# Attention and a feed-forward layer on one core: q and k of six batches by casting transfers in place of loads and casts on the engines, with a new order of all operations

## The chip, the cores and the metric

The kernel runs on one core of a Trainium2 chip. The core has five engines with a queue each: TensorE (PE in the profile; its weight loads are PEld), VectorE (DVE), ScalarE (ACT), GpSimd (POOL) and SyncE (SP), and 16 DMA engines that all queues share. Every engine runs its instructions in the order of its queue and waits on semaphores for the others. The metric is the device time of one execution in microseconds (us); smaller is better.

## The reference

Inputs are q, k and v, each of shape (8 batches, 12 heads, 448 rows, 64 columns), and the weights w_in (768 x 2048) and w_out (2048 x 768), all float32.

```python
scores = scale * np.matmul(q, k.transpose(0, 1, 3, 2))
attn = np.maximum(scores, 0.0) ** 2 / S
attn_out = np.matmul(attn, v)
...
x = attn_out.transpose(0, 2, 1, 3).reshape(B * S, H * D)
h = x @ w_in
g = h * (1.0 / (1.0 + np.exp(-1.702 * h)))
out = g @ w_out
```

So there is no softmax: the scores are clipped at zero and squared. The output has 3584 rows of 768 columns.

## The kernel before

All matrix work is in float16 with float32 sums. The work is cut into 24 attention units (8 batches of three units, a unit being two pairs of heads) and 8 feed-forward groups, one for each batch.

The whole order of the work is written out by hand (a planner's output) as a string of some 2,000 words, from line 431 on; `do` (line 404) calls one function for each word, and each engine's queue receives its instructions in the order of the words. A word is a name, its arguments, `@` the PSUM banks it takes, and `:` an engine (`a` ACT, `d` DVE, `p` POOL; some names have an engine as their home, for example the widening `v` POOL). The words that matter here:

- `Lq6`, `Lk6` (`load`, line 94): SP loads q or k of unit 6 in float32 into one staging tile each (pools qst and kst, one buffer). `Q6`, `K6` (`cast`, line 103) cast it on POOL, ACT or DVE into a float16 tile (pools q16 and k16, two buffers) whose two heads of a column block lie side by side. Units 0 and 6 to 23 take this way.
- `jq1`, `jk1` (`load_cast`, line 98): a DMA of POOL's queue loads q or k and casts on the way, as whole rows of 448 columns for each of the two halves, 256 packets in all. Units 1 to 5 take this way. `V3` does the same for v of unit 3 (pool v16, four buffers). `jwa0`, `jwb0` to `jwa3`, `jwb3` (`load_w_in`, line 374) load eight pieces of w_in and `jo0.0` to `jo1.1` (`load_w_out`, line 378) four pieces of w_out, on the same queue, 384 and 1024 packets each.
- `G3` (`sp_gate`, line 384): a small copy on SP that waits for the last piece of w_in, so that SP's later loads start behind it.
- `tq6`, `tk6` (`trans_pe`, line 112): PE turns a unit's q or k by multiplying with an identity matrix: 7 matmuls over the whole array (line 117) where the tile has heads side by side, 14 over half of it (line 122) otherwise. `eq6`, `ek6` (`trans_evac`, line 127) copy the result from PSUM.
- `s5.6@3.0` (`scores`, line 134): scores of unit 5, block 6, into banks 3 and 0; four matmuls of 64 x 64. `r`, `x`: clip (two halves, ACT or DVE) and square. `a5` (`attn_v`, line 164): the product with v, 28 matmuls. `e5.0`, `e5.1`: its two eviction halves into x of the batch (tile xb).
- `f0.14.0@3` (`m1`, line 202): two of the six matmuls of block 14 of the first feed-forward product of group 0. `g0.14` (`m1_gelu`, line 213): ACT reads the bank and writes the gelu into a float32 tile of pool gf, five buffers. `v0.14` (`m1_widen`, line 217): the widening, which scales a gf tile and writes it as float16 into its place in the tile ring, on POOL or DVE. With that the gf buffer is free. Groups 1 to 7 do the first product by a seven-product scheme (`u`, `t`, `b`, `g`, `v` with three arguments: product, copy, addition, gelu, widening).
- `p0.0` (`pair_product`, line 339): 8 matmuls of the second product for rows of the pair of tiles 0 and 1, which read ring blocks 0 to 7 and w_out; `p0.1` reads blocks 8 to 15. `A`, `S`, `T`, `W` are sums of operands on DVE for the seven-product scheme. `h`, `l` evict, `o` and `q26.0.1` store.

Within the first 60 us the order is: units 0 to 2 (batch 0) of the attention while the weights land, then the first feed-forward product of group 0 between the scores of units 3 to 5, then `u1...` and `p0.0`. From there attention of the next batches and feed-forward of the one before run interleaved to the end.

Of the kernel before, what the change touches and what calls it, by code (L numbers as in the profile page):

```python
# [8 lines left out]
F32 = mybir.dt.float32  # L9
# [6 lines left out]
def kernel(  # L16
# [31 lines left out]
    for name, bufs in (("cst", 1), ("kst", 1), ("qst", 1), ("k16", 2), ("q16", 2), ("v16", 4),  # L48
                       ("kT", 3), ("qT", 3), ("at", 15), ("xb", 2),
                       ("T1", 1), ("T2", 1), ("T4", 1), ("gf", 5),  # L50
                       ("as0", 1), ("as1", 1), ("osb", 3)):
        pool(name, bufs)
# [3 lines left out]
    def new(tag, shape, dt, name=None):  # L56
        return pools[tag].tile(shape, dt, name=name or tag, tag=tag)

    def const(name, shape, dt=F16):
        return pools["cst"].tile(shape, dt, name=name)  # L60

    ident = const("ident", [128, 128])
    gate = const("gate", [1, 64])
# [26 lines left out]
    def quad(n, u):  # L90
        b, pr = divmod(u, NP)
        return src[n][b].rearrange("(a i s) (p j) d -> i (s p) a (j d)", a=2, i=NP, j=J)[pr]

    def load(n, u):
        units[u][n + "st"] = new(f"{n}st", [128, 2, S], F32)
        nc.sync.dma_start(out=units[u][n + "st"], in_=quad(n, u))

    def load_cast(n, u):
        x = new(f"{n}16", [128, 2, S], F16)
        nc.gpsimd.dma_start(out=x, in_=quad(n, u))  # L100
        units[u][n + "16"] = x
# [282 lines left out]
    def sp_gate(e, p, i):  # L384
        nc.sync.dma_start(out=gate[0:1, :], in_=win[i][127:128, 0, 0:64])

    with tc.manual_schedule():
# [4 lines left out]
               "G": sp_gate,  # L392
# [29 lines left out]
        def zeros(e, p, n):  # L422
# [8 lines left out]
            "Lq0 Lk0 z9@0 jq1 jk1 I V0 V1 z1 Q0:d z1 z1 z1 z1 z1 z1 tq0@1 K0:d eq0:a tk0@2 ek0 "  # L431
            "tq1@3 jk2 eq1 s0.1@4.5 jq2 s0.4@6.7 s0.5@0.1 r0.1.1 r0.1.0:d s0.0@2.3 jq3 r0.5.1 "
            "r0.5.0:d s0.6@5.4 r0.0.0 r0.0.1:d r0.6.0 s0.2@1.0 x0.5 r0.2.0 s0.3@2.3 tk1@5 r0.2.1 "
            "x0.1 r0.4.0 ek1 jk3 r0.3.0 x0.2 r0.6.1 s1.6@1.0 jwb0 s1.3@6.5 r0.3.1:d r1.6.0 jwa0 "
            "r1.6.1 x0.6 s1.2@2.4 s1.0@3.1 r1.3.0 x0.3 r1.2.0 s1.5@0.6 x0.0 r0.4.1 r1.5.0:d r1.2.1 "
            "s1.1@2.7 r1.0.1 r1.0.0:d tk2@0 r1.1.0 x0.4 s1.4@4.1 r1.3.1 tq2@3 ek2 r1.1.1 a0@2.5 jq4 "
            "eq2 x1.3:a x1.2 jk4 r1.5.1 r1.4.0:d tq3@0 e0.0:a V2 x1.0 s2.3@7.3 e0.1:a tk3@6 jwb2 "
            "eq3 r2.3.1 s2.2@4.2 r1.4.1 ek3 s2.1@5.0 jwa2 r2.3.0 x1.1 s3.3@3.1 r2.1.1 jwa1 s2.4@6.7 "
            "x1.6 r2.2.0 jwb1 x1.4 r3.3.1 x1.5 a1@0.4 r2.1.0 jk5 r2.4.1 r3.3.0:d r2.2.1 jq5 "
            "s2.0@1.5 r2.4.0:d s3.2@7.3 e1.1:a f0.1.0@2 V3 e1.0 r2.0.0 s2.5@6.4 r2.0.1 r3.2.1:d "  # L440
            "jwb3 s3.4@0.1 r3.2.0 f0.1.1 r2.5.1:d r2.5.0 f0.0.0@5 jwa3 x2.2 f0.0.1 r3.4.0 V4 x2.0 "
            "s2.6@3.7 r3.4.1 s3.0@4.6 r2.6.0 x2.1 tk4@0 V5 r3.0.1 f0.2.0@1 r3.0.0:d r2.6.1 jo0.0 "
            "f0.2.1 x2.3 x2.5:a s3.6@3.6 x2.4 x2.6 a2@4.7 jo1.0 r3.6.0 r3.6.1 jo1.1 x3.4 tq4@3 ek4 "
            "e2.0:a jo0.1 f0.3.0@6 e2.1:a x3.0 f0.3.1 x3.2:a S0.1 f0.0.2 V14 f0.3.2 S0.2 g0.0 "
            "f0.1.2 eq4 g0.3 f0.2.2 g0.1 x3.3 s3.1@0.4 v0.3 s4.3@7.5 g0.2 s4.1@3.6 v0.1:d f0.10.0@2 "
            "r4.1.1 f0.10.1 r3.1.1:d r4.3.0 f0.10.2 r3.1.0 v0.0:d f0.8.0@1 r4.3.1 f0.8.1 x3.1 g0.10 "
            "f0.8.2 v0.2:d r4.1.0 s4.6@6.4 S2.1 v0.10 s4.5@7.0 s3.5@5.2 r4.5.0:d r4.5.1 f0.4.0@3 "
            "g0.8 f0.4.1 r4.6.0:d f0.6.0@7 x3.6:a v0.8:d f0.4.2 r3.5.1:d f0.6.1 r4.6.1 x4.5 f0.6.2 "
            "r3.5.0 x4.1 tq5@0 g0.4 tk5@1 x3.5 g0.6 s4.2@6.2 eq5:a ek5 s4.4@4.5 a3@3.7 r4.4.1:d "
            "r4.2.0 G3 x4.3 r4.2.1 Lk6 s4.0@0.1 S1.1 s5.0@5.6 e3.1:a Lq6 f0.5.0@2 r4.0.0:d r4.4.0 "  # L450
            "f0.11.0@7 r5.0.1 x4.4 f0.5.1 r5.0.0 f0.5.2 x4.6 e3.0:a s5.5@0.4 s5.1@6.5 S2.2 g0.5 "
            "f0.7.0@3 r5.5.0:d r4.0.1 f0.7.1 v0.5 x4.2:a f0.11.1 x4.0 V7 f0.7.2 S2.4 r5.5.1 f0.11.2 "
            "S2.3 g0.7 f0.15.0@2 f0.15.1 v0.6:d r5.1.1 v0.7 S0.4 f0.15.2 r5.1.0 s5.3@0.1 g0.11 "
            "s5.4@4.3 a4@5.6 g0.15 v0.11:d r5.3.0 r5.4.1:d v0.15 r5.3.1 s5.2@7.2 s5.6@0.3 e4.0:a "
            "x5.3 V6 f0.12.0@1 r5.6.1 K6:d f0.14.0@5 v0.4 r5.2.1 f0.12.1 r5.6.0:d Lk7 x5.0:a "
            "u1.1.0@3 x5.1 u1.0.0@2 r5.2.0 x5.6 r5.4.0 f0.13.0@0 x5.5 u1.2.0@7 e4.1:a S3.1 x5.2:a "
            "f0.12.2 x5.4 f0.14.1 g0.12 a5@4.6 S3.3 Q6:d S1.2 Lq8 tq6@1 e5.0:a v0.12:d f0.13.1 T1.1 "
            "e5.1:a f0.14.2 t1.1.0:d tk6@4 g0.14 T1.2 f0.13.2 S0.3 u1.0.1@6 g0.13 S3.2 p0.0@5 "
            "t1.0.0 v0.13 eq6:a b1.0.1 v0.14 S1.4 u1.0.2 ek6:a S3.4 u1.1.1@0 g1.0.1 T1.3 u1.3.0@1 "
            "t1.0.2 b1.1.1 v1.0.1 u1.1.2 S1.3 g1.1.1 u1.0.4 W0.1 t1.1.2 u1.0.3 W2.1 t1.0.4 u1.1.4 "  # L460
            "K7 b1.0.3 u1.1.3 W1.1 g1.0.3 Lk8 f0.9.0@4 T1.4 t1.1.4 u1.0.6 v1.0.3 Q8:a b1.1.3 f0.9.1 "
            "v1.1.1 f0.9.2 b1.0.6 Lq7 u1.1.6 W3.1 g0.9 u1.3.1@6 g1.1.3 b1.1.6 v0.9 t1.2.0 u1.1.5 "
            "v1.1.3:d t1.3.0 A0.1@0 u1.2.1@4 g1.0.6 W2.3 u1.2.2 g1.1.6 v1.0.6 b1.2.1 tk7@0 t1.2.2 "
            "u1.0.5 b1.3.1 v1.1.6 W1.3 u1.3.2 g1.3.1 W0.3 g1.2.1 u1.2.4 v1.3.1 W3.2 t1.3.2 u1.3.3 "
            "t1.2.4 u1.2.3 A0.2@1 ek7:a u1.2.5 W3.3 g1.0.5 b1.2.3 u1.3.4 K8 v1.0.5 h0.0:d tq8@0 "
            "W2.2 u1.2.6 g1.2.5 Lk9 W1.2 eq8:a p0.1@2 v1.2.5 b1.2.6 W0.2 t1.3.4 v1.2.1 W2.4 "
            "s6.0@7.0 p0.2 r6.0.0 Q7 l0.1 g1.1.5 b1.3.3 r6.0.1 V8 s6.4@4.7 Lq9 W0.4 h0.2 s6.2@3.0 "
            "p0.3 A0.3 r6.2.0 r6.4.1 W3.4 r6.2.1 W1.4 r6.4.0 s6.5@3.7 v1.1.5:d tq7@0 r6.5.0 A0.4 "
            "p0.4 r6.5.1 eq7 x6.2:a x6.5 s6.6@4.3 x6.0 h0.4 s6.3@7.0 Q9 r6.6.1 u1.3.5 r6.3.1:d "
            "r6.3.0 tk8@3 l0.3 g1.3.5 p0.5 K9:p Lq10 r6.6.0:d x6.4:a ek8 v1.3.5 Lk11 x6.3:a "  # L470
            "s7.4@0.7 l0.5 s6.1@1.4 u1.3.6 r7.4.0 r6.1.1:d o1 r7.4.1 x6.6 s7.0@3.5 s7.1@0.4 r6.1.0 "
            "p0.6 b1.3.6 r7.0.1 x6.1 r7.1.0 r7.0.0 x7.4 s7.3@7.1 r7.1.1 s7.2@6.5 l0.6 a6@0.3 r7.2.0 "
            "x7.1 o0 r7.3.0 A2.1@0 r7.2.1 s7.6@4.2 x7.0 r7.3.1 s8.4@6.7 V10 tq9@5 r7.6.0 r7.6.1:d "
            "tk9@1 Q10 e6.1:a r8.4.0:d p2.0@4 eq9:a ek9 K11:p r8.4.1:d x7.2:a s8.2@2.3 x7.6 "
            "s7.5@6.5 Lk10 p2.1@1 r7.5.1 r7.5.0:d Lq11 e6.0:a x7.3 x7.5:a r8.2.0:d s8.1@7.5 a7@6.0 "
            "r8.2.1:d r8.1.1 r8.1.0 A2.2@1 h2.0 x8.1 s8.6@2.3 s8.3@5.7 e7.0:a p2.2 r8.3.0:d e7.1:a "
            "K10:p r8.6.0 r8.6.1:d r8.3.1 l2.1 V13 s9.0@6.5 Lk12 x8.6:a s8.0@0.2 x8.3 s8.5@3.7 p2.3 "
            "r8.0.0:d r8.0.1 r9.0.1 x8.2 r8.5.1 x8.0 tk11@0 r8.5.0 u2.1.0@2 x8.4 ek11:a x8.5 a8@5.7 "
            "h2.2 A2.3 Q11:a A2.4 K12:p s9.3@3.0 e8.0 p2.4 r9.3.1 Lq12 r9.3.0:d e8.1:a Lk13 r9.0.0 "
            "T2.1 u2.1.1@5 h2.4 T2.3 g1.3.3 s9.2@0.3 T2.2 s9.4@7.6 r9.2.0 l2.3 p2.5 v1.3.3 r9.4.0 "  # L480
            "r9.2.1:d t2.1.0 T2.4 g1.2.3 u2.0.0@0 l2.5 g1.3.6 v1.2.3 u2.1.2 r9.4.1:d g1.2.6 o3 "
            "tq11@7 x9.3:a v1.2.6 p2.6 Q12:d t2.1.2 b2.1.1 t2.0.0 Lq14 tk10@3 eq11 g2.1.1 u2.0.2 "
            "l2.6 ek10:a K13:p u2.0.1@4 v1.3.6:d u2.1.4 Lk15 b2.0.1 o2 u2.1.3 A4.1@0 g2.0.1 tq10@6 "
            "t2.0.2 t2.1.4:d u2.2.0@7 v2.0.1 b2.1.3 u2.3.1@1 v2.1.1:d u2.1.5 g2.1.3 eq10 u2.2.1@3 "
            "v2.1.3 t2.2.0:d g2.1.5 u2.0.4 Q14:a b2.2.1 v2.1.5 u2.0.3 A4.2@1 t2.0.4 Lq13 s9.1@6.2 "
            "g2.2.1 u2.2.2 b2.0.3 r9.1.1 v2.2.1 u2.1.6 g2.0.3 t2.2.2:d u2.0.6 v2.0.3 b2.1.6 "
            "u2.3.0@2 x9.2 g2.1.6 u2.2.4 t2.3.0:d v2.1.6 u2.2.3 t2.2.4 b2.3.1 u2.3.2 r9.1.0 b2.2.3 "
            "g2.3.1 u2.0.5 x9.1 t2.3.2 u2.2.6 v2.3.1 b2.0.6 g2.2.3 u2.3.3 g2.0.5 V9 b2.2.6 u2.3.4 "
            "x9.0:a v2.2.3:d v2.0.5 s9.5@5.6 t2.3.4:d s10.6@4.0 u2.2.5 r10.6.1 r9.5.0:d r9.5.1 "
# [141 lines left out]
```

## Time and profile before

| | |
|---|---|
| median of 3 runs | 374.8 us (373.97 to 374.81) |
| profiled execution | 374.8 us |
| its span, first to last instruction | 373.0 us |
| busy: PE, DVE, ACT, POOL | 365.6, 321.5, 297.3, 114.3 us |
| POOL's casting loads of q, k and v | 5, 5 and 24, of 224 KB |
| SP's loads of q and k | 19 and 19, of 448 KB |
| casts of q and k: POOL, ACT, DVE | 25 (26.4 us), 7 (6.7 us), 6 (4.2 us) |
| matmuls | 3830 |

A row of the profile's groups gives the line, the engine, the operation, the tile written and the tiles read, their shapes, the number of instructions, the busy time and the mean of one; behind the bar stand the idle time of the engine just before them and what ended it. The timeline lists merged instructions: start, length, engine, line, operation, tiles, number. The list of waits gives the engine and line that waited, what it waited for, the total, the number of waits and the longest. In the list of DMA queues, q0 is POOL's queue and q1 SP's; behind the number of packets stand MB and the share of the 16 DMA engines' time that the packets took, which can pass 100% as packets overlap. In the list of DMA issues the last number is the time from issue to landing.

### The profile page before, as it was taken

The page shows a single profiled execution, that of the slowest core. Times are in us where ns is not written, and L with a number is a line of the kernel's source. Part 1 is how long each engine was busy: PE and PEld are TensorE (multiplying, and loading weights), DVE is VectorE, ACT ScalarE, POOL GpSimd, SP SyncE. Part 2 cuts the span into 40 slices and gives each one's busy share as a digit, 9 for nine tenths or more (in the row PEclk, how much of TensorE's full clock was granted, in tenths as well). Part 3 has the DMA queues.
Part 4 walks back from the last instruction along what each step waited for, and adds up shares of the span by engine and source line. Part 5 has one row for each costly group of instructions (what it writes and reads, how often), then busy time and mean ns, then how long its engine had stood idle before and what let it go on. Part 6 is the DMA issues. An engine that isn't in the chain of part 4 may idle for free.

```text
span 373.0 us, 9514 instructions
## 1 busy us (share of the span) xinstructions
PE 365.6 (98%) x3830; PEld 252.9 (68%) x3830; DVE 321.5 (86%) x602; ACT 297.3 (80%) x568; POOL 114.3 (31%) x164
## 2 busy tenths in 40 slices
PE   8899999999999999999999999999999999999995
PEld 4444568855589555886568965599568855788663
DVE  3999999999999998898899699978998889767762
ACT  3999989999988999789978997899994897636310
POOL 6464523452334424231341322335400410012000
PEclk9999999999999999999999999999999999999999
DMA  9999999357673437360572524620520301110344
GB/s 195 171 188 206 238 232 232 135 138 203 166 196 99 120 62 209 112 160 2 134 199 34 177 28 114 183 37 2 95 43 2 86 2 41 45 44 16 71 99 114
DMA packets 31981, 43.16 MB, mean 116 GB/s; under 512 B 2368, under 2 KB 28608, under 8 KB 31936
## 3 DMA queue, kind: packets, MB, share of 16 engines
q1 hardware_dynamic: 14928, 28.06, 25.7%
q0 software_dynamic: 16608, 14.09, 25.2%
q8 instruction: 30, 0.49, 0.5%
q10 hardware_dynamic: 400, 0.39, 0.4%
q14 instruction: 15, 0.12, 0.1%
HBM read 45.61 MB, written 11.01 MB: 152 GB/s over the span
## 4 chain that ended last, share of the span: by engine, by line
PE 95%; DVE 3%; ACT 1%; issue 0%
PE ox L188 35%; PE hx L188 30%; PE sc L141 10%; PE av L172 8%; PE ht L208 5%; PE tr L117 4%; PE zp L426 1%; DVE at L85 1%; DVE at L152 1%; PE tr L122 1%; ACT at L154 1%; DVE kT L80 0%; DVE qT L80 0%; DVE osb L357 0%; DVE wT L417 0%
## 5 line engine op out<-in xcount | busy, mean ns | idle before, releaser
L154 ACT ACTIVATE at<-sc 128x448 f16<-128x448 f32 x229 | 112.2, 567 | 10.6 <-PE sc L141 9.9
L198 POOL TENSOR_SCALAR ring<-gf 128x448 f16<-128x448 f32 x87 | 53.7, 617 | 151.0 <-ACT gf L195 144.0
L188 PE MATMUL ox<-wout,ring 128*128 128x384 f16 x448 | 80.3, 326 | 0.0
L188 PEld LDWEIGHTS <-ring 128*128 128x128 f16 x568 | 53.0, 98 | 37.5 <-issue 7.6
L152 DVE TENSOR_SCALAR at<-sc 128x448 f16<-128x448 f32 x107 | 63.9, 617 | 5.8 <-PE sc L141 5.6
L85 DVE TENSOR_TENSOR at<-at 128x896 f16<-128x896 f16 x107 | 65.5, 636 | 1.7 <-ACT at L154 1.6
L188 PEld LDWEIGHTS <-win 128*128 128x128 f16 x672 | 63.8, 98 | 4.4 <-issue 2.1
L85 DVE TENSOR_TENSOR gf<-hx,gf 128x448 f32<-128x448 f32 x84 | 50.8, 620 | 9.9 <-PE hx L188 5.2
L160 ACT ACTIVATE at<-at 128x896 f16<-128x896 f16 x61 | 57.7, 960 | 0.5
L188 PE MATMUL hx<-xb,win 128*128 128x224 f16 x504 | 57.0, 259 | 0.0
L195 ACT ACTIVATE gf<-gf 128x448 f32<-128x448 f32 x84 | 47.2, 578 | 11.5 <-DVE gf L85 11.3
L141 PE MATMUL sc<-qT,kT 64*64 64x448 f16 x672 | 50.2, 359 | 1.6 <-DVE kT L80 1.1
L188 PEld LDWEIGHTS <-winS 128*128 128x128 f16 x504 | 48.0, 98 | 3.1 <-issue 1.3
L76 ACT ACTIVATE gf<-hx 128x448 f32<-128x448 f32 x60 | 31.8, 541 | 13.4 <-PE hx L188 11.4
L188 PE MATMUL ox<-wT,asum 128*128 128x384 f16 x224 | 40.6, 327 | 0.0
L188 PE MATMUL hx<-T,winS 128*128 128x224 f16 x336 | 39.7, 259 | 0.0
L172 PE MATMUL av<-at,v 64*64 64x448 f16 x672 | 36.2, 350 | 0.1
L141 PEld LDWEIGHTS <-kT 64*64 64x64 f16 x672 | 17.1, 105 | 23.9 <-issue 17.3
L188 PEld LDWEIGHTS <-asum 128*128 128x128 f16 x224 | 20.8, 98 | 16.6 <-issue 3.4
L357 DVE SCALAR_TENSOR_TENSOR osb<-ox,osb 128x384 f32<-128x384 f32 (+1 forms) x44 | 23.8, 541 | 5.9 <-PE ox L188 5.7
L78 ACT ACTIVATE osb<-ox 128x384 f32<-128x384 f32 x26 | 13.1, 503 | 19.6 <-PE ox L188 16.8
L172 PEld LDWEIGHTS <-v 64*64 64x64 f16 x672 | 20.4, 107 | 11.6 <-issue 1.5
(61 smaller groups left out, 426.0 us busy)
## 6 DMA issues: line engine op xcount, KB each, us to landing
out_dram<-osb SPq DMA_DIRECT2D x52, 192.0 KB, 3.0
qst<-in_q_dram SPq DMA_DIRECT2D x19, 448.0 KB, 4.5
kst<-in_k_dram SPq DMA_DIRECT2D x19, 448.0 KB, 4.2
v<-in_v_dram POOLq DMA_DIRECT2D x24, 224.0 KB, 5.0
win<-in_moe_w_in_dram POOLq DMA_DIRECT2D x8, 384.0 KB, 9.7
wout<-in_moe_w_out_dram POOLq DMA_DIRECT2D x4, 768.0 KB, 20.6
q<-in_q_dram POOLq DMA_DIRECT2D x5, 224.0 KB, 5.9
k<-in_k_dram POOLq DMA_DIRECT2D x5, 224.0 KB, 5.4
```

The lines of the kernel that those rows point to most:

```text
L76: nc.scalar.activation(out=o, in_=i, func=AF.Copy)
L85: eng[e].tensor_tensor(out=o, in0=x, in1=y, op=op)
L141: nc.tensor.matmul(out=sc[a][c, 0:S], lhsT=st["kT"][r, j, c], rhs=st["qT"][r, :, c], start=True, stop=True)
L152: nc.vector.tensor_scalar(out=o, in0=i, scalar1=0.0, scalar2=None, op0=ALU.max)
L154: nc.scalar.activation(out=o, in_=i, func=AF.Relu)
L160: nc.scalar.activation(out=at, in_=at, func=AF.Square)
L172: nc.tensor.matmul(out=av[s][64 * a:64 * a + 64, 0:S], lhsT=v16[r, a, 64 * j:64 * j + 64], rhs=at[r, a, :], start=(j == 0), stop=(j == J - 1))
L188: nc.tensor.matmul(out=o, lhsT=lhs(i), rhs=rhs(i), start=start and i == 0, stop=i == n - 1, skip_group_check=True)
L195: nc.scalar.activation(out=o, in_=i, func=AF.Gelu_apprx_sigmoid, scale=1.0 / SC)
L198: eng[e].tensor_scalar(out=o, in0=i, scalar1=SC, scalar2=1.0, op0=ALU.mult, op1=ALU.mult)
L208: nc.tensor.matmul(out=hp[g, f][:, 0:S], lhsT=w[:, i, fo:fo + 128], rhs=xts[g][:, i, :], start=i == 0, stop=i == NK - 1)
L357: nc.vector.scalar_tensor_tensor(out=o, in0=x, scalar=1.0 / SC, in1=o, op0=ALU.mult, op1=ALU.add)
```

## The change

Units 6 to 23 no longer go through a staging tile and a cast. `load_cast` gets a second form for them: two DMAs on POOL's queue, one for each half, that cast and at the same time write the seven column blocks of 64 of a row into the tile with the heads side by side, so that a row of a half is written in seven pieces of 128 bytes. `trans_pe` then takes the path of 7 matmuls, as before. The pools of q16 and k16 get four buffers instead of two, the staging pools go, unit 0's loads by SP are staged in the tile ring, which nothing else uses yet, and the gate goes. All words are in a new order.

```diff
-    for name, bufs in (("cst", 1), ("kst", 1), ("qst", 1), ("k16", 2), ("q16", 2), ("v16", 4),
+    for name, bufs in (("cst", 1), ("k16", 4), ("q16", 4), ("v16", 4),
                        ("kT", 3), ("qT", 3), ("at", 15), ("xb", 2),
                        ("T1", 1), ("T2", 1), ("T4", 1), ("gf", 5),
...
     def load(n, u):
-        units[u][n + "st"] = new(f"{n}st", [128, 2, S], F32)
+        o = "kq".index(n) * 4 * S
+        x = ring.rearrange("p f c -> p (f c)")[:, o:o + 4 * S].bitcast(F32)
+        units[u][n + "st"] = x.rearrange("p (a c) -> p a c", a=2)
         nc.sync.dma_start(out=units[u][n + "st"], in_=quad(n, u))
 
     def load_cast(n, u):
-        x = new(f"{n}16", [128, 2, S], F16)
-        nc.gpsimd.dma_start(out=x, in_=quad(n, u))
+        if n == "v" or u < 2 * NP:
+            x = new(f"{n}16", [128, 2, S], F16)
+            nc.gpsimd.dma_start(out=x, in_=quad(n, u))
+        else:
+            x = new(f"{n}16", [128, J, 2, D], F16)
+            for a in range(2):
+                nc.gpsimd.dma_start(
+                    out=x[:, :, a, :], in_=quad(n, u)[:, a, :].rearrange("p (j d) -> p j d", d=D))
+            x = x.rearrange("p j a d -> p (j a d)")
         units[u][n + "16"] = x
...
-    def sp_gate(e, p, i):
-        nc.sync.dma_start(out=gate[0:1, :], in_=win[i][127:128, 0, 0:64])
```

Of the words, the start of the old order with its loads, and the new order from the last w_in piece to the words that the prediction speaks of:

```diff
-            "Lq0 Lk0 z9@0 jq1 jk1 I V0 V1 z1 Q0:d z1 z1 z1 z1 z1 z1 tq0@1 K0:d eq0:a tk0@2 ek0 "
-            "tq1@3 jk2 eq1 s0.1@4.5 jq2 s0.4@6.7 s0.5@0.1 r0.1.1 r0.1.0:d s0.0@2.3 jq3 r0.5.1 "
...
+            "Lq0 Lk0 z9@0 jq1 jk1 jk2 V0 jq2 z1 Q0:d z1 z1 I z1 z1 z1 z1 jq3 tq0@1 K0 jk3 eq0:a "
+            "tk0@2 V1 tq1@3 ek0 jwb0 eq1 s0.4@4.5 s0.5@6.7 jwa0 s0.1@0.1 r0.4.0:d r0.4.1 s0.2@2.3 "
...
+            "r1.1.1 V3 r1.0.1 x0.6 s1.5@1.0 jwb3 s2.2@6.7 r1.4.1 x0.2 r1.5.1 x0.4 a0@4.5 jwa3 "
+            "r2.2.1 x1.1 r1.5.0 jq6 r1.4.0 x1.0 tk3@0 eq3:a x1.4 s2.3@7.1 ek3 r2.2.0 V4 s2.4@3.2 "
+            "x1.3:a x1.2 x1.5 x1.6 a1@0.6 jq8 r2.4.1 e0.1:a e0.0 r2.3.1 jo0.0 r2.3.0:d e1.0:a "
+            "s2.0@2.5 s3.4@4.1 e1.1:a r2.4.0:d f0.0.0@7 V5 r3.4.0 f0.0.1 r3.4.1:d r2.0.1 s2.5@0.6 "
+            "jo1.0 x2.3 r2.0.0 s3.2@3.4 s2.1@1.5 r2.5.1:d r3.2.0 f0.3.0@2 jo1.1 r2.5.0 r2.1.0:d "
+            "f0.3.1 r2.1.1 f0.1.0@6 x2.2 jk7 r3.2.1 s2.6@3.0 x2.0 s3.3@1.5 r2.6.0 f0.1.1 x2.4 "
+            "r2.6.1 tq4@4 r3.3.1 x2.1 tk4@3 jk6 x2.5:a x2.6 a2@0.5 ek4 r3.3.0 eq4 s3.0@3.1 jo0.1 "
+            "e2.1:a e2.0 f0.2.0@4 r3.0.0 f0.2.1 r3.0.1:d jq7 x3.3:a f0.0.2 x3.4 s3.6@5.0 s4.5@3.1 "
+            "g0.0 f0.3.2 r4.5.0:d r3.6.1 f0.1.2 r4.5.1:d f0.2.2 g0.1 x3.0 s4.3@7.3 s3.1@0.1 "
+            "r4.3.0:d f0.8.0@6 r3.1.0 f0.8.1 r3.1.1:d g0.3 f0.8.2 r4.3.1 r3.6.0:d v0.3 s4.1@7.0 "
+            "g0.8 s3.5@1.2 S2.1 tq5@3 jk8 r3.5.1 x3.6 tk5@5 r3.5.0 s4.0@6.2 x3.5 f0.10.0@1 r4.0.1 "
+            "f0.10.1 x3.1 r4.0.0 jk9 f0.10.2 g0.2 v0.8:d f0.6.0@2 r4.1.1:d g0.10 f0.4.0@6 r4.1.0 "
+            "f0.4.1 v0.10:d ek5:a f0.4.2 S0.1 v0.2 f0.6.1 eq5 f0.6.2 x3.2:a x4.1 jq9 s4.6@4.0 "
+            "s4.2@1.7 S1.1 a3@5.3 g0.6 r4.6.1 S1.2 r4.2.1 r4.6.0:d v0.0 s5.0@2.0 r4.2.0 v0.1:d "
+            "f0.7.0@7 e3.1:a V8 S2.2 f0.7.1 r5.0.1 v0.6:d f0.11.0@4 V10 g0.4 x4.5 f0.7.2 e3.0:a "
+            "f0.11.1 x4.6 r5.0.0 f0.11.2 S2.3 g0.7 s4.4@1.3 s5.1@0.6 x4.2 s5.5@5.2 r4.4.0 f0.15.0@7 "
+            "S3.1 r4.4.1 f0.15.1 x4.3 r5.1.1 f0.15.2 x4.4:a r5.1.0:d f0.12.0@1 f0.12.1 v0.7:d g0.15 "
+            "f0.14.0@3 S1.3 f0.14.1 r5.5.0 S3.2 f0.12.2 g0.11 x4.0 f0.14.2 r5.5.1 x5.0 f0.5.0@6 "
+            "g0.12 f0.5.1 S1.4 g0.14 s5.4@0.7 s5.2@5.4 v0.14 a4@2.1 r5.4.0:d r5.4.1 r5.2.1 S3.3 "
+            "x5.5:a x5.1 s5.6@3.0 v0.15:d V6 f0.9.0@7 r5.6.0 S0.2 tq6@4 e4.1:a v0.4 S0.3 f0.5.2 "
+            "r5.6.1 f0.13.0@3 v0.12 x5.4:a r5.2.0:d s5.3@1.0 f0.13.1 x5.6 e4.0:a f0.9.1 r5.3.0:d "
+            "x5.2:a f0.13.2 u1.1.0@5 r5.3.1:d f0.9.2 x5.3 t1.1.0 a5@2.1 g0.5 v0.11:d S3.4 u1.2.0@0 "
+            "e5.0:a e5.1 V7 g0.13 u1.0.0@6 T1.1 jq10 t1.2.0 u1.0.1@2 T1.2 t1.0.0 T1.3 u1.1.1@1 "
+            "v0.5:d u1.1.2 b1.0.1 v0.13 S0.4 p0.0@3 t1.1.2 b1.1.1 g1.0.1 W2.1 eq6:a u1.1.4 v1.0.1 "
...
```

Over the whole string, 36 words of loading by SP and 36 of casting go and 36 of casting loads come; 11 evictions of xb move from ACT to DVE, 6 widenings from POOL to DVE and 3 squares from ACT to DVE, and PE's words are the same in number, in another order.

## The prediction

> **What bounds the kernel now.** I read the page first: busy time, clock, chain, DMA queues.
>
> ```profile
> PE 365.6 (98%) x3830; PEld 252.9 (68%) x3830; DVE 321.5 (86%) x602; ACT 297.3 (80%) x568; POOL 114.3 (31%) x164
> ...
> PEclk9999999999999999999999999999999999999999
> ...
> q0 software_dynamic: 16608, 14.09, 25.2%
> ...
> PE 95%; DVE 3%; ACT 1%; issue 0%
> ...
> v<-in_v_dram POOLq DMA_DIRECT2D x24, 224.0 KB, 5.0
> ```
>
> TensorE (PE) is the chain, at full clock. Busy does not prove that it moves at its own step, so the timeline of its matmuls comes next.
>
> ```profile
> 47.90 0.55 PE L141 MATMUL sc<-qT,kT 64*64 64x448 f16 x8
> 48.38 1.31 PE L208 MATMUL ht<-xb,win 128*128 128x448 f16 x6
> 49.52 1.22 PE L188 MATMUL hx<-xb,win 128*128 128x224 f16 x11
> ```
>
> From start to start: 6 ht matmuls take 1.14 us (0.19 each); the 8 score matmuls, two words of four, 0.48 us: twice 0.19 and 0.10 for the change of tile shape. Adding such steps over the old word list up to u1.1.0 (the row at 49.52) gives 43.4, so PE had waited 6.1 us by then, all in the first 22 us; behind it nearly every gap is a change of shape. So nothing that the change takes off ACT, DVE or POOL can gain after 22 us, and it gains at most these 6 us.
>
> Then POOL, whose queue the change fills: first what it waited for between 20 and 45 us, then its timeline.
>
> ```profile
> POOL win L375 <- DMA win<-in_moe_w_in_dram: 2.2, 1, 2.2
> POOL v L100 <- DMA win<-in_moe_w_in_dram: 1.2, 1, 1.2
> POOL wout L379 <- DMA k<-in_k_dram: 1.2, 1, 1.2
> POOL win L375 <- DMA v<-in_v_dram: 0.5, 1, 0.5
> ```
>
> ```profile
> 34.75 1.75 POOL L379 DMA_DIRECT2D wout<-in_moe_w_out_dram  x2 [1.23 <-DMA k<-in_k_dram]
> 36.72 0.88 POOL L379 DMA_DIRECT2D wout<-in_moe_w_out_dram  x1 [0.22 <-issue]
> 38.79 0.70 POOL L100 DMA_DIRECT2D v<-in_v_dram  x1 [1.20 <-PE tr L122]
> 39.56 0.56 POOL L198 TENSOR_SCALAR ring<-gf 128x448 f16<-128x448 f32 x1
> ```
>
> No load of a weight reads a k or a v, and each weight has its own tile, yet POOL waits for such landings. Numbering its DMAs shows why: the 26th (the second wout) waits for the 18th (jk5), the 21st (a win) for the 13th (V2), the 22nd for the 14th. **A DMA of POOL waits until the eighth before it has landed**, and POOL stands still meanwhile: v0.3, written between words that PE ran at about 32, came at 39.56. Nothing needed it, so PE lost nothing. The last wout's landing, from the DMA view of its issue at 36.72, and the queue without other traffic (19 to 33 us):
>
> ```profile
> wout<-in_moe_w_out_dram POOLq DMA_DIRECT2D x1, 768.0 KB, 26.5
> ```
>
> ```profile
> q0 software_dynamic: 2903, 2.68, 121.7%
> ```
>
> It landed at 63.2. Queue 0 moved 2903 packets in 14 us on 16 engines, 77 ns each, one DMA after the other; a 256-packet load so takes 1.28 us.
>
> **The change, part by part.** *Removed:* 36 loads on SP and the gate (SP keeps its stores, which waited for DVE's osb, not for loads: nothing), and casts: 25 on POOL (13.7 + 12.7 us), 6 of ACT's 7 net (6.7 less 0.95), 5 of DVE's 6 (4.2 less 0.7). I price them at nothing: PE's matmuls hide them, and no engine was late. Between nothing and a gain of 6 us, if ACT and DVE work in the first 22 us was what PE waited for; but only batches 2 to 7 lose casts, so nothing.
>
> *Moved:* the word counts take 11 evictions of xb from ACT to DVE (6.8 us), 6 widenings from POOL to DVE (2.5) and 3 squares (1.9); DVE stays near 329 of 373 us; without that slack it would cost up to the 11 us. PE's matmuls are the same in number; changes of shape 134 against 136 (0.2 us). The start (two loads earlier, K0 on ACT, identity after five DMAs instead of two): between -3 and +3, taken as nothing. The tail is the same to within one eviction moved to DVE (0.05 us).
>
> *Added on POOL:* 72 DMA issues. Row v has 745 ns (256 packets), row wout 879 (1024); for 896 packets 0.85, so 61 us. POOL is idle two thirds of the time: nothing in sum; it counts where something is queued behind.
>
> *Added on queue 0:* each load becomes 1792 packets of 128 B written, 256 B read. No row shows such a packet. By bytes it costs a seventh of v's 80 ns, 11.4; by packets 80. A load is then T = 1.28 to 8.96 us. I take the geometric middle, 30 ns, T = 3.36, since v is the nearest row and nothing tells whether it is bound by bytes or by packets.
>
> The Trainium skill's page "DMA: Bandwidth & Descriptors" (Specifications) says that line rate needs 512 B and that smaller writes are read back first. If that doubled my packet, T would be 6.7 and the time 458 by the first rival's sum below, an estimate from that page. Its section "Why small descriptors are slow" charges three bus cycles beside eight for 256 B; that makes 15.7 ns of the by-bytes bound, T 1.8, and the time 396, again an estimate. No run here shows either.
>
> *The added wait.* POOL's new order: ... jwa3 **jq6** V4 **jq8** jo0.0 V5 jo1.0 jo1.1 **jk7 jk6** jo0.1 **jq7** v0.3 **jk8 jk9** v0.2 **jq9** v0.0 V8 V10 v0.14 V6 v0.4 v0.12 V7 jq10 v0.13. Up to jo0.1 stand the 28 DMAs of the old order, plus four loads. jo0.1 landed at 63.2; less 2 us, since the SP loads that shared the engines are gone (22% of their time in 46 to 62 us), plus 4T = 13.4: 74.6. The eighth DMA behind it is jq9's second half. Behind that, on POOL, stands v0.0: 0.85 for the issue, 0.57 for v0.0: done at 76.0.
>
> Who waits for v0.0? The gelus write gf, five buffers. Between the words g0.14 and v0.14 five tiles are alive: g0.4, g0.15, g0.11, g0.12, g0.14. One of them must sit where g0.0 sat, whichever way buffers are dealt out. So ACT, in order, can't pass g0.14 before v0.0: 76.0 + 0.57 = 76.6. PE needs that gelu to empty bank 3 for s5.6@3.0. Without a wait PE would be at s5.6 at 49.8: the old order ran u1.1.0 at 49.52 behind 42 scores and 39 f words; the new has 40 and 41 and one change of shape fewer before s5.6 (-0.38 + 0.76 - 0.10). Loss: **26.8 us**.
>
> What is late next? p0.0, 8.8 us of matmuls later, reads ring blocks 0 to 7; v0.4 ends near 81, in time. V6 lands near 92, while a6, by the same steps at 86.4 without the loss, comes at 113. From there queue 0 has two loads and a v to move, 8 us, per unit of some 16 us of PE. Nothing adds.
>
> *The clock.* PE would stand 20 to 25 us. The first 16 zp matmuls, from a standing start, took 5.24 us, 16 like ones at the end 2.76: up to 2.5 us lost in coming back, less where ACT and DVE refill anyway. I take 1.2.
>
> **Sum.** The profiled execution took 374.8 us at a span of 373.0, equal to the median of the three runs (374.8). 374.8 + 26.8 + 1.2 = **402.8 us**. Bounds of this case: T = 1.28 gives a loss of 18.5 (393); T = 4.5 gives 31.3 and 2.5 for the clock (409). Even T = 0 leaves 13.4, because v0.0 now stands eight DMAs behind the last weight.
>
> **Rivals.**
> 1. *Queue 0 becomes the bound.* Behind jo0.1 stand 32 loads and some 18 v (23 us). jk20 is the last load; by the steps, and the 8 us that the old order had waited by then, its turn comes at 242, and 131 us of the span are left. The landing, 61.2 + 36T + 23, passes that turn (242 plus the loss, 13.4 + 4T) from T = 5.4 on. With T = 7: 336 + 131 + 1.8 around the span, 469 us; with 8.96, 540. For: the packets are seven times as many. Against: 80 ns is a price for 896 B. Chance 0.13.
> 2. *POOL isn't held, but the queue is late.* If widenings could go on, V6 behind eight loads would land at 91.9 against a6 at 86.4: 5.5 us late, 380 us. Against: v0.3's 39.56. Chance 0.08.
> 3. *Faster.* POOL isn't held and T is at most 2.7, the point from which V6 is no longer late; then the earlier loads cut half of the 6.1 us that PE waits at the start: 371.7. For: four buffers instead of two let POOL issue early. Against: the four waits shown above. Chance 0.05.
> 4. *The split writes are no split*: were the packets still whole rows, T is 1.28 and the time 393; it lies in the forecast's bounds.
>
> The forecast has 0.71; 0.03 is left for within 0.3%, about what a measurement of this kernel can tell from no change. Faster 0.05, same 0.03, slower 0.92. The range 388 to 440 holds the forecast, a piece of the first rival and little of the second.
>
> **What would show it.** In the profile after: POOL's v0.3 near 59, v0.0 near 75; POOL rows that wait for DMAs q and k; ACT idle before a gelu with POOL's ring line as releaser; a hole of 20 us or more in PE between 45 and 80 and a lower PEclk there; queue 0 with some 82,000 packets and a share near 53% (64,512 packets of 30 ns on 16 engines, and the old 94 us of packet time, over 403). Each step fails by itself: T by the landing of q and k, the hold by v0.0's time, the place by PE's hole. Wrong would be a PE without a hole, or holes all along the span.

## The result and the profile after

The changed kernel takes 391.2 us (median of 3 runs, 390.3 to 391.6) against 374.8: 1.044 times as long, with a 95% interval of 1.041 to 1.048. The prediction said 402.8 and 388 to 440. The profiled execution took 390.3 us at a span of 388.6, 15.6 more than before. These lines of its page answer to those of before:

```profile
PE 369.8 (95%) x3830; PEld 254.8 (66%) x3830; DVE 325.5 (84%) x614; ACT 287.9 (74%) x551; POOL 156.7 (40%) x205
...
PEclk9999959999999999999999999999999999999999
...
q0 software_dynamic: 82272, 22.36, 58.2%
...
PE 83%; DMA 14%; ACT 1%; POOL 1%; issue 1%; DVE 0%; SPq 0%
...
q<-in_q_dram POOLq DMA_DIRECT2D x36, 112.0 KB, 4.2
```

ACT's busy time fell by 9.4 us, DVE's rose by 4.0 and POOL's by 42, and the chain, 95% PE before, now leads through DMAs for 14%. One slice of the clock row, 49 to 58 us, shows half speed: something stood still just there. POOL's timeline shows where it stood (start, length, engine, line, operation, tiles; in brackets the idle time before and its releaser; line 206 is the widening, 387 a w_out piece, 106 a split load):

```profile
46.61 0.90 POOL L387 DMA_DIRECT2D wout<-in_moe_w_out_dram  x1 [1.54 <-DMA wout<-in_moe_w_out_dram]
48.03 0.96 POOL L106 DMA_DIRECT2D q<-in_q_dram  x1 [0.52 <-DMA v<-in_v_dram]
51.62 0.98 POOL L106 DMA_DIRECT2D q<-in_q_dram  x1 [2.63 <-DMA wout<-in_moe_w_out_dram]
52.68 0.56 POOL L206 TENSOR_SCALAR ring<-gf 128x448 f16<-128x448 f32 x1
...
59.75 0.56 POOL L206 TENSOR_SCALAR ring<-gf 128x448 f16<-128x448 f32 x1
60.37 1.02 POOL L106 DMA_DIRECT2D q<-in_q_dram  x1
62.34 0.98 POOL L106 DMA_DIRECT2D q<-in_q_dram  x1 [0.95 <-DMA wout<-in_moe_w_out_dram]
63.40 0.60 POOL L206 TENSOR_SCALAR ring<-gf 128x448 f16<-128x448 f32 x1
```

The row at 62.34 is the second half of jq9: it waits for the last w_out piece, the eighth DMA before it, and behind it stands v0.0 (63.40). The widenings at 52.68 and 59.75 are v0.3 and v0.2. ACT's timeline has a gelu behind each of the three:

```profile
53.28 0.54 ACT L203 ACTIVATE gf<-ht 128x448 f32<-128x448 f32 x1 [10.86 <-POOL ring L206]
...
60.34 0.55 ACT L203 ACTIVATE gf<-ht 128x448 f32<-128x448 f32 x1 [1.64 <-POOL ring L206]
...
64.03 0.98 ACT L203 ACTIVATE gf<-ht 128x448 f32<-128x448 f32 x2 [2.71 <-POOL ring L206]
```

And PE waits for those gelus to empty its banks:

```profile
53.87 1.45 PE L149 MATMUL sc<-qT,kT 64*64 64x448 f16 x7 [9.73 <-ACT gf L203]
55.26 6.33 PE L216 MATMUL ht<-xb,win 128*128 128x448 f16 x22
...
64.63 1.51 PE L180 MATMUL av<-at,v 64*64 64x448 f16 x26 [2.35 <-ACT gf L203]
65.79 0.54 PE L149 MATMUL sc<-qT,kT 64*64 64x448 f16 x4
```

The last row is s5.6, whose place without a wait was 49.8: it stands 16.0 us late, the whole 15.6 of the span. The 22 ht matmuls between the holes take 6.33 us; in a run without a hole before them (the third experiment) the same 22 take 4.34. The windows give the reason (columns: us, then busy time of PE, PEld, DVE, ACT and POOL, the granted clock, DMA share, GB/s):

```profile
40.00:50.00 10.00, 4.15 (x45) 1.79 (x38) 5.39 (x12) 2.42 (x6) 6.93 (x8) 0.95 1.41 200
50.00:60.00 10.00, 6.13 (x22) 2.42 (x22) 3.50 (x7) 4.97 (x10) 5.74 (x7) 0.53 1.65 189
60.00:70.00 10.00, 7.65 (x77) 4.03 (x76) 5.71 (x10) 6.95 (x13) 6.83 (x10) 1.00 1.94 169
```

The clock was 0.53 between 50 and 60 us; in the trace it is halved from 49.1 to 59.3. It cost nothing here, because PE would only have come sooner to the hold that ended with v0.0.

### The profile page after: what moved, and what is told of

It reads as the page before. It is cut to its first block, busy times and chain, and to the rows that moved or that the text cites. A ratio compares the mean times of both kernels' runs of the same rounds, so it can differ in the third digit from the quotient of the medians.

```text
span 388.6 us, 9528 instructions
## 1 busy us (share of the span) xinstructions
PE 369.8 (95%) x3830; PEld 254.8 (66%) x3830; DVE 325.5 (84%) x614; ACT 287.9 (74%) x551; POOL 156.7 (40%) x205
## 3 DMA queue, kind: packets, MB, share of 16 engines
q0 software_dynamic: 82272, 22.36, 58.2%
q1 hardware_dynamic: 5104, 11.54, 10.8%
## 4 chain that ended last, share of the span: by engine, by line
PE 83%; DMA 14%; ACT 1%; POOL 1%; issue 1%; DVE 0%; SPq 0%
PE ox L196 34%; PE hx L196 29%; PE sc L149 8%; PE av L180 7%; DMA wout<-in_moe_w_out_dram 7%; PE tr L125 4%; DMA v<-in_v_dram 3%; DMA q<-in_q_dram 3%; DMA ring<-in_k_dram 1%; PE ht L216 1%; ACT at L162 0%; POOL q L106 0%; ACT k L75 0%; DVE kT L79 0%; POOL ring L206 0%
## 5 line engine op out<-in xcount | busy, mean ns | idle before, releaser
L206 POOL TENSOR_SCALAR ring<-gf 128x448 f16<-128x448 f32 x81 | 50.9, 628 | 143.5 <-ACT gf L203 125.8
L160 DVE TENSOR_SCALAR at<-sc 128x448 f16<-128x448 f32 x106 | 62.9, 617 | 18.0 <-PE sc L149 17.2
L84 DVE TENSOR_TENSOR at<-at 128x896 f16<-128x896 f16 x110 | 67.5, 635 | 3.1 <-ACT at L162 2.3
L149 PE MATMUL sc<-qT,kT 64*64 64x448 f16 x672 | 52.2, 361 | 10.5 <-ACT gf L203 9.7
L84 DVE TENSOR_TENSOR gf<-hx,gf 128x448 f32<-128x448 f32 x84 | 51.1, 618 | 11.4 <-PE hx L196 6.6
L168 ACT ACTIVATE at<-at 128x896 f16<-128x896 f16 x58 | 56.0, 967 | 3.1 <-DVE at L160 2.9
L106 POOL DMA_DIRECT2D q<-in_q_dram x36 | 35.8, 994 | 29.6 <-PE tr L125 22.2
L75 ACT ACTIVATE gf<-hx 128x448 f32<-128x448 f32 x63 | 33.4, 545 | 13.4 <-PE hx L196 10.9
L149 PEld LDWEIGHTS <-kT 64*64 64x64 f16 x672 | 17.9, 105 | 33.0 <-issue 26.0
L180 PE MATMUL av<-at,v 64*64 64x448 f16 x672 | 37.1, 350 | 2.5 <-ACT gf L203 2.3
L106 POOL DMA_DIRECT2D k<-in_k_dram x36 | 35.5, 987 | 7.1 <-PE tr L125 4.3
## 6 DMA issues: line engine op xcount, KB each, us to landing
win<-in_moe_w_in_dram POOLq DMA_DIRECT2D x8, 384.0 KB, 12.3
wout<-in_moe_w_out_dram POOLq DMA_DIRECT2D x4, 768.0 KB, 13.4
```

What stands on the lines that cost most here:

```text
L75: nc.scalar.activation(out=o, in_=i, func=AF.Copy)
L84: eng[e].tensor_tensor(out=o, in0=x, in1=y, op=op)
L106: nc.gpsimd.dma_start(out=x[:, :, a, :], in_=quad(n, u)[:, a, :].rearrange("p (j d) -> p j d", d=D))
L149: nc.tensor.matmul(out=sc[a][c, 0:S], lhsT=st["kT"][r, j, c], rhs=st["qT"][r, :, c], start=True, stop=True)
L160: nc.vector.tensor_scalar(out=o, in0=i, scalar1=0.0, scalar2=None, op0=ALU.max)
L168: nc.scalar.activation(out=at, in_=at, func=AF.Square)
```

## The experiments

Three theories could explain the 16 us. A: the hold, that is POOL's DMAs wait for the eighth before, and the widenings behind them wait along. B: the new order of words, POOL or not. C: the small packets, which slow the queue. Each run was compared with the kernel before on the same chip (374.5 to 374.9 us).

**Widenings off POOL.** First three, then seven words get the mark of DVE:

```diff
-  ... v0.3 ... v0.2 ... v0.0 ...
+  ... v0.3:d ... v0.2:d ... v0.0:d ...
```

> The changed kernel with three widenings of the first feed-forward group, v0.3, v0.2 and v0.0, on DVE instead of POOL; order and loads untouched. Theory A (the hold): POOL's DMAs still stand still for the eighth before them, but these three no longer stand behind them, so ACT's first three waits (10.9, 1.6 and 2.7 us in the changed kernel) go; v0.14, v0.4 and v0.12 are still behind waiting DMAs (65.6 to 67.3 us in the changed kernel) and p0.0, due near 58.5, waits for them. About 384 us, with PE's hole starting near 58 instead of 54. Theory B (the new order of words costs the time by itself, POOL or not) and theory C (the small packets slow the queue and everything that lands behind them): 391 us as the changed kernel, with the hole where it was.

```diff
-  ... v0.14 ... v0.4 ... v0.12 ... v0.13 ...
+  ... v0.14:d ... v0.4:d ... v0.12:d ... v0.13:d ...
```

> As the run before, with v0.14, v0.4, v0.12 and v0.13 on DVE too: seven widenings off POOL. Theory A: nothing that PE needs before p0.0 is left on POOL; what remains is v1.0.1, some 7 us late, and about 3 us more work on DVE: 376 to 380 us. Theories B and C: still 391 us; if A holds and DVE can't take the work, 382 or more.

Measured: 386.7 us (1.033 [1.028, 1.037]) and 383.0 (1.022 [1.019, 1.024]). The holes moved as A says. PE's one hole in the first, and ACT's wait in the second, in their timelines:

```profile
66.73 3.52 PE L196 MATMUL hx<-xb,win 128*128 128x224 f16 x18 [9.99 <-ACT gf L203]
```

```profile
68.73 0.54 ACT L75 ACTIVATE gf<-hx 128x448 f32<-128x448 f32 x1 [5.33 <-POOL ring L206]
```

PE passed the place of the old hole without a stop and stood at 56.7 in the first, at 64.6 in the second, each time for the next widening still on POOL. So PE's order of words and the packets, B and C, fall as the cause of the large hole. One part of B stays inside A: of the three widenings only v0.3 was POOL's in the kernel before, where v0.2 and v0.0 are DVE's, as they are again in the runs of the old order below. It was the new words that put those two on POOL, behind the loads, so the hole comes of the two choices together. Both times came out some 3 us above what I had written: 18 hx matmuls in 3.52 us are about twice their 1.72 (0.0955 each), so behind each hole there is a stretch at half clock, and I had not priced it: 3.9 us long in the first run and 4.6 in the second, it costs about 2 of the 3 us. The time of the second also fits the reading "382 or more", that DVE can't take the work, but its trace doesn't: PE's waits for DVE there came to 0.7 us, its wait behind POOL's widening to 4.7.

**Only POOL's queue in another order.** The w_out pieces go ahead of all split loads but jq6, the loads behind widenings:

```diff
-  ... jq6 V4 jq8 jo0.0 V5 jo1.0 jo1.1 jk7 jk6 jo0.1 jq7 v0.3 jk8 jk9 v0.2 jq9 v0.0 V8 V10 v0.14 ...
+  ... jq6 V4 V5 jo0.0 jo1.0 jo1.1 jo0.1 v0.3 jq8 v0.2 v0.0 jk7 v0.14 V6 V7 v0.4 v0.12 jk6 v0.13 jq7 ...
```

> The changed kernel with POOL's queue alone in another order: the four w_out pieces right behind V5, ahead of all split loads but jq6, and each further split load behind a widening that PE needs earlier (v0.3 jq8 v0.2 v0.0 jk7 v0.14 ...). Every load is still split, with the same packets, and every other engine keeps its order. Theory A: the hold goes, jo0.1 lands some 6 us earlier (three split loads fewer ahead of it), nothing waits: 373 to 376 us. Theory B: 391 us. Theory C: most of the 16 us stays, since the queue moves the same packets: 385 or more.

Measured: 383.5 us (1.023 [1.019, 1.026]); a miss. The large hole is gone, but small ones are there: PE stood 2.4 us until 41.6 (v0.3 stood behind the last piece, whose own issue waited) and 3.8 us in three holes between 70 and 83. There POOL's issues were too dense:

```profile
70.00:80.00 10.00, 7.91 (x85) 6.78 (x83) 8.70 (x16) 8.33 (x16) 9.65 (x12) 1.00 1.13 85
```

POOL is busy 9.65 of 10 us: a split load costs it 2 x 0.99 us, and a widening behind it is late by that much, without any DMA being waited for.

**The old order, split loads alone.** The words of SP's loads become split loads, casts and gate go (pools and the staging of unit 0 as in the changed kernel):

```diff
-  ... Lk6 ... K6:d ... Lq6 ... Q6:d ...
+  ... jk6 ... jq6 ...
```

> The kernel before in its own order of words, with the casting loads alone: where SP loaded q or k of units 6 to 23, POOL's two split DMAs stand, the casts and the gate are gone, turning takes the same path. Pools as in the changed kernel. Theory A: in the old order these loads stand behind the w_out pieces and few widenings are behind them while the weights land: 374 to 378 us. Theory B: 374.8 us, the old order's time. Theory C: the small packets bring their loss in any order: 385 us or more.

Measured: 385.4 us (1.028 [1.025, 1.030]); a miss by 8 us. PE's timeline has one large hole:

```profile
59.87 0.93 PE L125 MATMUL tr<-ident,q 128*128 128x128 f16 x7 [5.90 <-DMA q<-in_q_dram]
```

That is q of unit 6. On SP its load ran beside the w_out pieces; on POOL's one queue it stands behind all four. Its last packet ended at 59.5, and PE was ready for it at 54.0. Half clock behind the hole lasted 3.5 us more. So the change leaves a choice: loads ahead of the pieces hold the pieces and, through the rule of eight, POOL; loads behind them come late themselves.

**Packets or number of DMAs.** The first run keeps two DMAs a load and writes whole rows, the second makes it one DMA, both in the new order:

```diff
-                    out=x[:, :, a, :], in_=quad(n, u)[:, a, :].rearrange("p (j d) -> p j d", d=D))
+                    out=x.rearrange("p j a d -> p (j a d)")[:, a * S:(a + 1) * S], in_=quad(n, u)[:, a, :])
```

> The changed kernel, in its own order and still with two DMAs a load, but each half is written as whole rows (128 packets of 896 bytes a DMA in place of 896 of 128), so the heads of a block don't lie side by side and q and k of batches 2 to 7 are turned with misplaced columns: the scores of these batches aren't the reference's. Theory A1 (what holds POOL is the number of DMAs, which the rule of eight counts; the packets only set how long each takes): the four loads ahead of the last w_out piece took some 8.4 us of the queue in the changed kernel and would take 5 us, so v0.0 comes 3 to 4 us earlier and the loss of 16.4 us falls to 12 to 14: 387 to 389 us. Theory A2 (the small packets are what costs): 376 to 380 us.

```diff
-        if n == "v" or u < 2 * NP:
-            x = new(f"{n}16", [128, 2, S], F16)
-            nc.gpsimd.dma_start(out=x, in_=quad(n, u))
-        else:
...
+        x = new(f"{n}16", [128, 2, S], F16)
+        nc.gpsimd.dma_start(out=x, in_=quad(n, u))
```

> The changed kernel, in its own order, but every load of q and k of all units is one DMA of whole rows, as units 1 to 5 have it, and is turned by 14 matmuls over half of the array instead of 7 over the whole. The output is the reference's. Theory A1: with half as many DMAs the eighth behind the last w_out piece is V7, after v0.3, v0.2, v0.0, v0.14, v0.4 and v0.12, so the hold is gone but for a wait for the third piece (v0.0 near 50 us, due 49.8); the turning costs 0.03 to 0.12 us of PE for each of 36 loads, 1 to 4 us: 376 to 381 us. Theory A2: as the run before, lower by no more than the issues. Theory B (the order): 391 us.

Measured: 390.8 us (1.042 [1.040, 1.044]) and 386.6 (1.031 [1.029, 1.033]). With a third of the packets on queue 0 (26,976) the time stays: theory A2 falls. The packets in the trace show why the gain stayed small: from the first packet of one DMA on the queue to the first of the next, the four loads took 4.6 us in all, and in the changed kernel 6.0 (not the 8.4 that I had put down before the run); the w_out pieces took 3.8 us each in both. So the last piece landed only 1.2 us earlier. And the little that v0.0 gained (61.72 against 63.40) PE did not get:

```profile
52.86 1.46 PE L149 MATMUL sc<-qT,kT 64*64 64x448 f16 x7 [8.87 <-ACT gf L203]
58.66 7.18 PE L216 MATMUL ht<-xb,win 128*128 128x448 f16 x22 [4.35 <-ACT gf L203]
```

The second hold ended at 58.7, and the 22 ht matmuls behind it ran at half clock for 7.18 us instead of 4.34, past v0.0; s5.6 came at 67.5. With one DMA a load the hold shrinks to 3.0 us, as A1 says (what is left is a wait for v0.3, at 42.45 behind the issues of the pieces; v0.0 at 51.31 holds nothing), but the time is 5.6 us above the top of what I expected. Two things were left out: half clock behind the hold again, some 2 us, and the turning, which the timeline of that run prices:

```profile
104.13 1.47 PE L189 MATMUL ox<-wT,asum 128*128 128x384 f16 x8
105.53 0.58 PE L123 MATMUL tr<-ident,k 128*64 128x128 f16 x14
106.05 1.32 PE L189 MATMUL hx<-xb,win 128*128 128x224 f16 x12
```

From start to start the 8 ox matmuls take 1.40 us (1.30 is 8 x 0.1625) and the 14 turning ones 0.52, where 7 over the whole array take 0.39 and no gap: 0.23 us more for a turning between two matmuls of the whole array, in the change of tile shape.

**Loads when they are due.** From the third run, jk6 into an idle stretch, other loads later, v0.3 on DVE:

```diff
-  ... jo0.1 v0.3 jq8 v0.2 v0.0 jk7 v0.14 V6 V7 v0.4 v0.12 jk6 v0.13 jq7 v1.0.1 jk8 v1.1.1 v0.9 jk9 V8 ...
+  ... jo0.1 v0.3:d jq8 v0.2 v0.0 jk7 jk6 v0.14 v0.4 v0.12 V6 v0.13 V7 v1.0.1 v1.1.1 jq7 v0.9 v1.1.3 v1.0.3 jk8 ...
```

> The kernel of loads after widenings (383.5 us) with POOL's queue thinned where it was full: its 70 to 80 us slice had POOL busy 9.65 of 10 us with issues of 0.99 us, and ACT waited for widenings there. jk6 goes into the idle stretch ahead of v0.14, nine other loads 5 to 15 us later, each still some 10 us ahead of its turning, and v0.3, which stood behind the last w_out piece, goes to DVE. Theory A: PE's holes at 38.8 (2.6 us and 2 us of lower clock behind it) and at 70 to 82 (4 us) go: 374 to 377 us. If the packets themselves cost PE time (theory C), 381 or more.

From the old order, q and k of unit 6 ahead of the pieces, v0.3 on DVE:

```diff
-  ... V5 jo0.0 jo1.0 jo1.1 jo0.1 ... v0.3 ... jk6 jq6 ...
+  ... V5 jq6 jk6 jo0.0 jo1.0 jo1.1 jo0.1 ... v0.3:d ...
```

> The old order with split loads (385.4 us), whose one large hole was PE's turning of q of unit 6, held 5.9 us by a load that stood behind the w_out pieces; here q and k of unit 6 go ahead of the first piece, and v0.3 to DVE. Theory A: the hole of 6 us and 2 us of lower clock behind it go, the pieces land some 3 us later, near 57.5, in time for the second product at 58: 375 to 379 us. If something else of the split loads costs the time, 383 or more.

Measured: 379.8 us (1.013 [1.011, 1.015]) and 376.7 (1.0048 [1.0033, 1.0063]). In the first, the hole at 41.6 is gone and the mean clock is 1.00, but ACT still waits 7.8 us for widenings between 64 and 86, and PE loses 3.7 us between 60 and 90: a miss by 3, half cured. The second came as expected: no hold is left. What it still loses, ACT's timeline shows:

```profile
66.79 0.54 ACT L75 ACTIVATE gf<-hx 128x448 f32<-128x448 f32 x1 [1.20 <-POOL ring L206]
...
72.88 0.54 ACT L203 ACTIVATE gf<-hx 128x448 f32<-128x448 f32 x1 [0.68 <-POOL ring L206]
...
75.72 0.54 ACT L75 ACTIVATE gf<-hx 128x448 f32<-128x448 f32 x1 [1.49 <-POOL ring L206]
```

**The two loads in the way, three loads ahead of the last piece, and the turning alone.**

```diff
-  ... v1.1.1 jq7 v0.9 v1.0.6 v1.1.6 v1.3.1 v1.0.5 jk9 v1.2.5 v1.2.1 ...
+  ... v1.1.1 v0.9 v1.0.6 v1.1.6 v1.3.1 jq7 v1.0.5 v1.2.5 v1.2.1 jk9 ...
```

> The kernel with the old order and q and k of unit 6 early (376.7 us), with two loads moved behind widenings that ACT waited for: its PE was level with the kernel before at 60 us and lost 2 us between 67 and 78, where ACT waited 1.2, 0.7 and 1.5 us for POOL widenings that stood behind the issues of jq7 and jk9 (2 us each). jq7 goes behind v1.3.1 into an idle stretch of POOL, jk9 behind v1.2.1. Theory A (issues on POOL in front of widenings): 374.5 to 375.5 us, the kernel before within 0.3%. If the loads cost by anything but their place: 376.7 us again.

Measured: 374.6 us beside 374.5 for the kernel before on that chip: 1.000 [0.999, 1.001]. Lines of its page:

```profile
PE 365.6 (98%) x3830; PEld 252.7 (68%) x3830; DVE 318.3 (85%) x599; ACT 291.9 (78%) x561; POOL 158.0 (42%) x210
...
PEclk9999999999999999999999999999999999999999
...
q0 software_dynamic: 82272, 22.36, 60.3%
```

All 82,272 packets and all 72 issues are there, and the time of the kernel before: theory C falls, and the split loads cost nothing where they and the widenings are placed for it. Theory B isn't wholly excluded: in the new order the best time was 379.8 us, and whether its last 5 us go with more thinning wasn't tried.

```diff
-  ... jq6 V4 jq8 jo0.0 V5 jo1.0 jo1.1 jk7 jk6 jo0.1 jq7 v0.3 jk8 jk9 v0.2 jq9 v0.0 V8 ...
+  ... jq6 V4 jo0.0 V5 jo1.0 jo1.1 jo0.1 jq7 v0.3 jk8 jk9 v0.2 jq9 v0.0 jq8 jk7 jk6 V8 ...
```

> The changed kernel with three of the four split loads ahead of the last w_out piece (jq8, jk7, jk6) moved behind v0.0; jq6 stays, since q of unit 6 is turned first, and the eighth DMA behind the last piece is still the second half of jq9. Theory A with the measured price of a load: these three took 2.1 and 3.7 us of the queue, so the last piece lands and v0.0 comes 5.8 us earlier, near 57.6; the loss falls from 16.4 to about 10.5 us: 385 us. If the time of the loads in the queue isn't what sets the hold: 391 us.

Measured: 387.2 us (1.034 [1.033, 1.036]). v0.0 came at 59.15, 4.25 us earlier instead of 5.8. Counted by the first packets again, the three loads had taken 4.2 us of the queue in the changed kernel, and not the 5.8 that I had put down, so A holds with the right price. But s5.6 came at 62.37, only 3.4 us earlier; the rest went to the clock, for the 22 matmuls of 4.34 us took 7.13:

```profile
52.57 7.13 PE L216 MATMUL ht<-xb,win 128*128 128x448 f16 x22 [3.19 <-DMA wout<-in_moe_w_out_dram]
```

The releaser in the bracket is a landing of the same moment; the ht matmuls read no w_out, and v0.2, done at 51.95, with the gelu behind it came just before them.

The last run takes the unsplit `load_cast` of the second diff above into the old order with q and k of unit 6 early:

> The old order with q and k of unit 6 early (376.7 us), but each load is one DMA of whole rows and is turned by 14 matmuls over half of the array. The hold plays no part here, so this prices the turning: with the 0.10 us into and 0.13 us out of the other tile shape that the run of whole rows in the new order shows, 36 loads cost 7 to 8 us of PE; the single issue on POOL gives back 1 to 2 us: 381 to 384 us. If 14 matmuls cost what was expected at first (0.03 to 0.12 us): 376 to 379 us.

Measured: 379.5 us (1.013 [1.012, 1.015]). Its PE line shows the price of turning by 14, against 365.6 in the run without waits:

```profile
PE 370.2 (98%) x4082; PEld 250.9 (67%) x4082; DVE 318.2 (84%) x599; ACT 293.0 (78%) x561; POOL 113.4 (30%) x174
```

That is 4.6 us, 0.13 a load, and the time lies between the two forecasts: less than I expected, since beside scores or another turning, where many of them stand, part of the change of shape is paid anyway. So laying heads side by side in the transfer is worth 4.6 us of PE over whole rows. That is what the casts on the engines also bought, behind PE.

No version here beats both kernels; the best equals the kernel before. Not tried: whether work taken off ACT and DVE in the first 22 us, where PE still waits some 6 us, would gain.

## Why the prediction was right, and where its sizes were off

*Nothing to gain after 22 us.* Right, and shown by the run at 1.000: there SP's 36 loads and 36 casts are gone, and PE's time is what it was.

*A DMA of POOL waits for the eighth before it.* Right: the second half of jq9 waited for the last w_out piece, and v0.0 stood behind it. The runs with widenings on DVE and with one DMA a load moved the hold as this says. Why it is the eighth, no run here shows. That last wait was only 0.95 us, though: ahead of it POOL had waited 2.63 us for the second piece and 2.47 at 55.72, where by the numbering the third had to land (the view names PE there, but the landing in the first experiment). Between 55.72 and v0.0 it issued six DMAs of about 1 us. With the last piece 3 us earlier, v0.0 would still have come within 1 us of where it came.

*Who waits for v0.0.* Right in the chain gf, ACT, bank, PE. But I named only the last of three waits; the longest, 10.9 us, was for v0.3, which came at 52.68 where I had 59. So PE stood from 44.1 and again from 62.3, 12.1 us in sum, and not once for 20 or more.

*The landing of the last piece.* This is the mis-sized term: 74.6 predicted, 62.3 by the wait for it. Three parts make up the 12.3, each from the first packet of one DMA on the queue to the first of the next. T was taken as 3.36 us; jq6 took 1.8, jq8 1.3 and jk7 with jk6 3.0, which is 6.0 instead of 13.4: -7.4. The w_out pieces took 15.2 us instead of 20.7 before, and 15.4 in each run of the old order in which SP's loads are gone, so the 2 us that I took off should have been 5.5: -3.5. And the queue was 1.7 us ahead at the end of the w_in pieces (36.0 against 37.7). The two loads of v between took 0.4 more. (The lower bound of T, 1.28, came from 80 ns a packet, where the row beside it gives 77 and so 1.23; a load of whole rows took 1.15.) The price of a packet was not what failed in T: its records last 32 ns, I took 30. But they overlap, so that one went by in 13 ns, which shows in the queue's share over three microseconds of split loads alone (62 to 65 us, after):

```profile
q0 software_dynamic: 3677, 0.46, 242.3%
```

By the Trainium skill's page "DMA: Bandwidth & Descriptors", section "Why small descriptors are slow", T came to 1.8 us and the time to 396; the loads took 1.5 on average, so that was the nearer of its two rules. The rule under Specifications, doubled packets and 458 us, is not what this case shows.

*The loss.* 26.8 us predicted, 16.0 measured. v0.0 is done 12.0 us earlier than in the sum (64.0 against 76.0); 1.2 of that is lost again, as ACT had two gelus and PE 26 av matmuls between v0.0 and s5.6.

*The clock.* 1.2 us predicted, nothing in the changed kernel, where the slow stretch lay inside the hold. But it is no small term: in two experiments (387.2 and 390.8 us) it cost 2.8 us behind the last hole. Without that, the runs that shorten the hold can't be read.

*The issues.* 0.85 us each taken, 0.99 measured, 10 us in sum over the 72. "POOL is idle two thirds of the time" was true of the whole span and wrong between 70 and 80 us, as the run with loads after widenings showed. In the changed kernel the price above 0.85 cost nothing: the wait for the last piece covered it.

*The rivals.* Queue 0 never became the bound (T under 5.4). POOL was held, so the second and third fall; the first experiment adds that the third's gain at the start doesn't come even where nothing holds PE until 56.7: s5.6 came at 49.95 there, beside 49.8 at the old order's pace. Packets of whole rows, the fourth's, were run: 390.8, near its 393, with an interval that overlaps that of the small ones, so T between 1.15 and 1.5 us hardly enters.

## What to carry to other kernels

Moving a load from one queue to another moves its place in line, too: write out the new queue, number its DMAs, and for each engine instruction behind a DMA ask which landing that DMA must wait for. Put work that others wait for ahead of such DMAs or on another engine, and place each load between its neighbours' deadlines; here that alone was worth 11.4 us in the new order (391.2 to 379.8) and 10.8 in the old (385.4 to 374.6). And when a stall of PE is shortened, count the half clock behind it before you count the gain.

## What the runs showed of the hardware

- Packets of 128 B cost far less than their records say: 32 ns each, but 2.4 run at once on an engine (the 242% above), so a split load took 1.5 us, where a load of whole rows took 1.15.
- The wait for the last w_out piece ended 0.6 us after the last of its packets (61.7 and 62.3). The 16 engines don't end together: the first packet of the load behind it started at 60.0, while the piece ran on to 61.7.
- Each of the ten holes of PE of 2.4 to 10 us brought half clock, and behind the last hole of a stretch it lasted 3.4 to 5.8 us more; the hole of 2.35 us before s5.6 in the changed kernel and those of up to 1.7 us brought none. The stretches at half clock lasted 3.41, 6.83, 10.24 or 17.07 us, that is one, two, three or five times 3.41, and behind the shortest holes they began only when PE was already running again (41.6 and 42.1 us in the third run). The Trainium skill's page "TensorE: Matmul & The Clock Gate", Part 1, gives a window of about 3.4 us for either change; here holes of 2.4 us were enough for the drop, and the way back took up to 5.8 us.
- Between matmuls of the whole array, 14 turning matmuls over half of it cost 0.10 us on the way in and 0.13 on the way out; the Trainium skill's page "TensorEngine Tiling (Array Packing)", section "Key Properties", says that a change of tiling mode drains the engine, which fits.
